# Sigmoid attention with a gated convolution: rounding of q and k in the DMA, tap products on GpSimd, due times anew

## The chip, the cores and the metric

The kernel runs on one core of one Trainium2 chip. The metric is the device time of one execution in microseconds, as the median of several runs. The engines are named as in the profile: PE is TensorE, PEld its weight loads, DVE is VectorE, ACT is ScalarE, POOL is GpSimd, SP is SyncE, which here only issues DMAs.

## What is computed

Attention with a sigmoid in place of the softmax, for 8 batches, 12 heads, 448 tokens and a head size of 64, and behind it a projection that is gated by a causal convolution of 5 taps over the tokens:

```python
scores = scale * np.matmul(q, k.transpose(0, 1, 3, 2)) - np.log(S)
attn = 1.0 / (1.0 + np.exp(-scores))
x = heads side by side of np.matmul(attn, v)          # [8, 448, 768]

for k in range(K):                                     # K = 5, x padded with zeros in front
    gate_pre += conv_w[k][None, None, :] * xp[:, k:k + S, :]
gate = 1.0 / (1.0 + np.exp(-gate_pre))
val = x @ w_val
return (gate * val @ w_out).astype(np.float32)
```

All inputs and outputs are fp32.

## The kernel before

**Tiling.** The 96 heads are taken in 48 pairs: pair i has two heads of 64 rows on the 128 partitions. Two pairs make a "two" j (24 of them), and three twos a batch (6 pairs of heads, 768 channels). Tokens lie along the free dimension. The first batch has no product of its own: its 448 tokens are dealt out to the other seven as an eighth segment of 64 tokens, so that each of seven batches has 512 tokens (line 654 loads that piece as x<-first_x).

**Precision.** PE multiplies fp32 slowly, so most operands are split in a rounded part and a remainder. The first 15 pairs are multiplied whole (`qk_single`, one L516 product). From pair 15 on, 33 pairs, q and k are split: `qk_hi` is the fp32r rounding of `qk_src`, `qk_lo` the remainder, and scores are three products. The sigmoid of the scores (L552) is split in two fp16 parts (`a`, L367 on ACT and L563 on DVE), v in `v_hi` and `v_lo`, x in `xs`, the gated value y in `g`, and the weights in `w_val_hi`, `w_val_lo`, `w_out_hi`, `w_out_lo`. The weights come as 64-bit words that three steps on DVE and ACT turn into fp32 (`w_words`), a maximum over each piece (`val_max`, `out_max`) gives its scale.

**Stages.** For each pair: load, split, scores (L516, and L539 for the last 64 tokens of both pairs of a two), sigmoid. For each two: the products with v (L602, L610) into `ps_a`, a copy of x out of PSUM, its maximum (`x_max`, L658), and the gate: the tap k=0 is a product x times conv_w that begins the gate; taps k=1 (and k=2 in the first gated batch) are added by DVE (L679); for the others (ADDED = 3, ADDED_FIRST = 2) a product is made in a `tap` tile, two instructions for a tile, and a DMA adds the tile to the gate (L683, on the POOL queue). Then a sigmoid of the gate (L685). For each batch: the maximum over x is spread over the partitions by a product with a diagonal (L702) and gives the scale of `xs`; then six `val` products (L753), y = value times gate (L777), the split of y in g, six `out` products (L753), and the stores.

**Order.** Nothing is left to a scheduler of the framework. Each piece of work is handed to `op` with the engines that may do it and a cost on each (`{"V": 0.31, "A": 0.45}`: DVE or ACT; G is POOL, S is SP), a due time, and the buffers it reads and writes. `Plan.issue` walks through planned time: an engine that is free takes the ready piece with the earliest due time, and DVE leaves a piece that ACT may also do if ACT is free within `AT["share"]`. The order found is written out for each engine; at run time each engine goes through its list in order and waits for semaphores. The due times are `tau(i)`, a clock of pairs, plus an offset from the table `AT`.

**Rings.** Buffers are reused in turn: `qk_src`, `qk_hi`, `qk_lo` have two each, `tap` two, `gate` four, `x` five, `ps_a` three, `ps_m` two, `w_words` three.

In the profile before, the casts are L361 (ACT) and L363 (DVE), the subtraction for qk_lo is L372 on POOL, and the tap products are `tap<-x,cw` at L367 on ACT.

Of the kernel before, what the change touches and what calls it, by code (L numbers as in the profile page):

```python
# [24 lines left out]
KT = 5  # L25
P = 128
# [52 lines left out]
    first=6.63, step=13.72, val=-77.5, val_step=60.94, out=57.5, out_step=597.15, w_max=-57.5,  # L79
    w_split=-155, load_qk_first=-152, load_qk=69.5, load_v=-40.5, split_hi=-2, split_lo=30,  # L80
    rest_first=95.5, rest=251, a_first=-174.5, a=-7, attend=-47.5, v_max=76.5, v_exp=14.5,
    v_split=-159.5, x=-174.5, x_max=-98, x_scale=-307, x_hi=52.5, x_lo=-185.5, x_step=2940.66, tap=51,
    scores=68.5, a_rest=85, a_rest_first=-72.5, tap_first=22, tap_pair=68.5, tap_step=56.18, gate=-110,
    product=63.5, y=-61.5, g_hi=186.5, g_lo=6, o=-97, share=0.3, w_load=-117,
# [39 lines left out]
class Op:  # L124
    __slots__ = ("ways", "prio", "emit", "deps", "n", "start", "end", "eng", "after", "size", "port", "then")

    def __init__(self, n, ways, prio, emit, size, port):
        self.n, self.ways, self.prio, self.emit, self.size, self.port = n, ways, prio, emit, size, port
        self.deps, self.after, self.then = set(), None, None
        self.start = self.end = self.eng = None  # L130
# [126 lines left out]
def attention_then_gate(  # L257
# [371 lines left out]
    def after(j):  # L629
# [318 lines left out]
```

## Time and profile before

| | |
|---|---|
| median of 3 runs | 579.03 us (578.53 to 579.27) |
| span of the profiled execution | 578.0 us |
| median less that span | 1.03 us |
| PE, DVE, ACT, POOL busy | 571.4, 428.4, 435.4, 138.2 us |
| DMA queue of SP (q1) | 56.37 MB, 28.9% of 16 engines |
| DMA queue of POOL (q0) | 31.46 MB, 29.4% of 16 engines |

The profile is one execution; its own time is its span and what lies around it, which for the median of the runs is 1.03 us. "Busy" is the time in which an engine has an instruction of its own; "idle before, releaser" in a group's row is how long the engine stood before these instructions and what let it go on. PE's matmuls overlap their neighbours, so a row's mean is longer than the step from one to the next.

### The profile page before, as it was taken

The page shows a single profiled execution, that of the slowest core. Times are in us where ns is not written, and L with a number is a line of the kernel's source. Part 1 is how long each engine was busy: PE and PEld are TensorE (multiplying, and loading weights), DVE is VectorE, ACT ScalarE, POOL GpSimd, SP SyncE. Part 2 cuts the span into 40 slices and gives each one's busy share as a digit, 9 for nine tenths or more (in the row PEclk, how much of TensorE's full clock was granted, in tenths as well). Part 3 has the DMA queues.
Part 4 walks back from the last instruction along what each step waited for, and adds up shares of the span by engine and source line. Part 5 has one row for each costly group of instructions (what it writes and reads, how often), then busy time and mean ns, then how long its engine had stood idle before and what let it go on. Part 6 is the DMA issues. An engine that isn't in the chain of part 4 may idle for free.

```text
span 578.0 us, 9459 instructions
## 1 busy us (share of the span) xinstructions
PE 571.4 (99%) x3592; PEld 280.2 (48%) x3592; DVE 428.4 (74%) x693; ACT 435.4 (75%) x579; POOL 138.2 (24%) x162
## 2 busy tenths in 40 slices
PE   9999999999999999999999999999999999999997
PEld 5343334455555555545555454554545555544444
DVE  1867999899977959888598886889777886760310
ACT  5677988879888869778697878788788897862112
POOL 0000203332424222243322333223322322110000
PEclk9999999999999999999999999999999999999999
DMA  8988677757484564825657364565635663355012
GB/s 327 355 279 267 174 210 188 203 120 184 124 215 83 146 157 141 207 58 155 136 158 176 102 169 96 166 156 155 169 74 168 155 133 74 72 128 129 2 37 74
DMA packets 39310, 88.44 MB, mean 153 GB/s; under 512 B 14944, under 2 KB 20448, under 8 KB 39264
## 3 DMA queue, kind: packets, MB, share of 16 engines
q0 software_dynamic: 8640, 31.46, 29.4%
q1 hardware_dynamic: 30624, 56.37, 28.9%
q8 instruction: 28, 0.46, 0.3%
q14 instruction: 18, 0.15, 0.1%
HBM read 43.96 MB, written 12.40 MB: 98 GB/s over the span
## 4 chain that ended last, share of the span: by engine, by line
PE 90%; DVE 5%; ACT 3%; DMA 1%; issue 1%; ACTq 0%; DVEq 0%
PE ps_m L753 54%; PE ps_a L516 15%; PE ps_a L610 14%; PE ps_a L539 3%; PE ps_a L602 2%; DMA gate<-tap 1%; ACT a_single L552 1%; DVE x_max L658 1%; DVE gate L679 1%; PE ps_m L800 1%; DVE a L563 1%; DVE w_words L389 1%; DVE out_max L415 0%; ACT tap L367 0%; ACT a L367 0%
## 5 line engine op out<-in xcount | busy, mean ns | idle before, releaser
L753 PE MATMUL ps_m<-g,w_out_hi 128*128 128x512 f16 (+1 forms) x516 | 150.5, 374 | 0.0
L753 PE MATMUL ps_m<-xs,w_val_hi 128*128 128x512 f16 x504 | 150.1, 379 | 0.0
L552 ACT ACTIVATE ps_a<-ps_a 128x896 f32<-128x896 f32 x112 | 99.3, 909 | 14.2 <-DVE v_exp L544 6.5
L563 DVE SCALAR_TENSOR_TENSOR a<-ps_a,a 128x896 f16<-128x896 f32 x96 | 100.8, 1082 | 7.0 <-ACT a L367 6.7
L372 POOL TENSOR_TENSOR qk_lo<-qk_src,qk_hi 128x448 fp32r<-128x448 f32 x66 | 75.2, 1151 | 119.8 <-ACT qk_hi L361 36.7
L753 PE MATMUL ps_m<-g,w_out_lo 128*128 128x512 f16 (+1 forms) x258 | 96.5, 374 | 0.0
L683 POOL DMA_DIRECT2D gate<-tap x60 | 53.5, 892 | 178.6 <-ACT tap L367 70.2
L753 PE MATMUL ps_m<-xs,w_val_lo 128*128 128x512 f16 x252 | 95.5, 379 | 0.0
L367 ACT ACTIVATE a<-ps_a 128x896 f16<-128x896 f32 x96 | 85.0, 927 | 0.2
L367 ACT ACTIVATE tap<-x,cw 128x512 f32<-128x512 f32 x120 | 82.2, 739 | 1.5 <-DMA gate<-tap 1.5
L753 PEld LDWEIGHTS <-w_out_hi 128*128 128x128 f16 x516 | 49.0, 98 | 59.6 <-issue 5.3
L753 PEld LDWEIGHTS <-w_val_hi 128*128 128x128 f16 x504 | 47.8, 98 | 61.1 <-issue 5.9
L777 DVE SCALAR_TENSOR_TENSOR y<-ps_m,y_scale,gate 128x512 f32<-128x512 f32 x42 | 29.9, 745 | 34.3 <-PE ps_m L753 34.3
L610 PE MATMUL ps_a<-a,v_hi 128*64 128x448 f16 x384 | 52.7, 354 | 0.0
L367 ACT ACTIVATE y<-ps_m,o_scale 128x512 f32<-128x512 f32 (+1 forms) x35 | 23.1, 678 | 38.0 <-PE ps_m L753 25.4
L552 ACT ACTIVATE a_single<-ps_a 128x896 f32<-128x896 f32 x56 | 48.0, 927 | 4.5 <-PE ps_a L516 4.1
L361 ACT CAST g<-y 128x512 f16<-128x512 f32 x28 | 17.2, 618 | 33.7 <-DVE y L777 32.9
L516 PE MATMUL ps_a<-qk_hi 64*128 64x448 f32 x198 | 39.8, 398 | 0.1
L753 PEld LDWEIGHTS <-w_out_lo 128*128 128x128 f16 x258 | 25.2, 98 | 29.2
L753 PEld LDWEIGHTS <-w_val_lo 128*128 128x128 f16 x252 | 24.7, 98 | 29.7
L516 PE MATMUL ps_a<-qk_single 64*128 64x448 f32 x180 | 39.0, 566 | 0.0
L610 PE MATMUL ps_a<-a_single,v_src 128*64 128x448 f32 x192 | 37.8, 543 | 0.0
(108 smaller groups left out, 752.9 us busy)
## 6 DMA issues: line engine op xcount, KB each, us to landing
gate<-tap POOLq DMA_DIRECT2D x60, 512.0 KB, 4.9
qk_src<-qk SPq DMA_DIRECT2D x33, 448.0 KB, 5.4
v_src<-vs SPq DMA_DIRECT2D x24, 448.0 KB, 4.3
out_t<-y SPq DMA_DIRECT2D x41, 224.0 KB, 3.1
qk_single<-qk SPq DMA_DIRECT2D x15, 448.0 KB, 5.9
w_words<-w_val SPq DMA_DIRECT2D x6, 768.0 KB, 8.1
w_words<-w_out SPq DMA_DIRECT2D x6, 768.0 KB, 5.4
x<-first_x SPq DMA_DIRECT2D x21, 68.0 KB, 4.2
```

The lines of the kernel that those rows point to most:

```text
L361: nc.scalar.copy(to, x)
L367: nc.scalar.activation(to, x, AF.Copy, scale=by)
L372: engines[eng].tensor_tensor(to, x, y, op=ALU.subtract)
L516: mm(b()[:, h, :S], k()[rows, at : at + P], q()[rows, :S], start=(n == 0), stop=(n == len(terms(i)) - 1))
L539: mm(b()[to, h, :S], x[n]()[rows, CW:], x[n]()[rows, :S], start=True, stop=True)
L552: nc.scalar.activation(to, b()[:, :, :S], AF.Sigmoid, bias=-math.log(S), scale=1.0 / math.sqrt(D))
L563: op({"V": 1.0}, t + 0.5, lambda e: nc.vector.scalar_tensor_tensor(part(1), p(), A_SCALE, part(0), op0=ALU.mult, op1=ALU.subtract), [b], [ ...
L602: mm(px()[to, p, :S], v()[rows, h * D : (h + 1) * D], x(s["a"])[rows, h, at : at + S], start=(j > 0 and n == 0), stop=(j == 0 and n == len ...
L610: mm(px()[to, p, :S], v()[:, o : o + D], x(st[2 * j + p]["a", c])[:, h, at : at + S], start=(j == 0 and c == 0 and n == 0), stop=(j > 0 an ...
L683: op({"G": 1.1}, at + AT["tap_step"] * k, lambda e, tap=tap: nc.gpsimd.dma_start(g(), tap(), accum_op=ALU.add), [tap], [g], 4 * P * T * 4, "")
L753: mm(po()[:, cs], w()[:, c, :], x(k)[:, cs], start=(c == 0 and j == 0), stop=(c == NC - 1 and j == 2))
L777: op({"V": 0.66}, t + AT["y"], lambda e: nc.vector.scalar_tensor_tensor(y(), po(), y_scale()[:, m : m + 1], gate()[:, m % 2, :], op0=ALU.m ...
```

## The change

Three things are changed.

- The rounded part `qk_hi` no longer is a cast of the loaded `qk_src` by DVE or ACT (two casts for each pair). A DMA on the POOL queue reads q and k from HBM a second time, fp32, and writes them as fp32r: one DMA for each of 33 pairs, 128 x 832 elements. `qk_src` is still loaded by SP, since the remainder and L539 read it.
- The products for the adding DMA, 120 of 128 x 512, are made by POOL with a `tensor_scalar` (times the weight, times 1.0), not by ACT. Their planned cost on POOL is `TAP_G`.
- The table `AT` has new values throughout, and due times are rounded to five places. `share`, 0.3 before, is 16.048: DVE takes a piece that ACT may do only if ACT is not free within 16 us of planned time.

```diff
+TAP_G = 0.65
...
 AT = dict(
-    first=6.63, step=13.72, val=-77.5, val_step=60.94, out=57.5, out_step=597.15, w_max=-57.5,
...
+    first=2.733, step=19.657, val=-59.018, val_step=26.262, out=78.183, out_step=3.48, w_max=-221.49,
...
-        self.n, self.ways, self.prio, self.emit, self.size, self.port = n, ways, prio, emit, size, port
+        self.n, self.ways, self.prio, self.emit, self.size, self.port = n, ways, round(prio, 5), emit, size, port
...
-        s["halves"] = (h, h.part()), (l, l.part())
-        for n, cs in enumerate((slice(0, S), slice(S, CW))):
-            op({"V": 0.31 - 0.03 * n, "A": 0.45 - 0.06 * n}, t + AT["split_hi"] + n, lambda e, cs=cs: copy(
-                e, h()[:, cs], x()[:, cs]), [x], [s["halves"][0][n]])
+        s["halves"] = (h,), (l, l.part())
+        op({"G": 1.0}, t + AT["split_hi"], lambda e: nc.gpsimd.dma_start(h()[:, :CW], qk[i][:, :CW]), [], [h], P * CW * 4, "")
         for n, cs in enumerate((slice(0, S), slice(S, CW))):
             op({"G": 1.13 - 0.14 * n}, t + AT["split_lo"] + n, lambda e, cs=cs: sub(
-                e, l()[:, cs], x()[:, cs], h()[:, cs].bitcast(F32)), [x, s["halves"][0][n]], [s["halves"][1][n]])
+                e, l()[:, cs], x()[:, cs], h()[:, cs].bitcast(F32)), [x, h], [s["halves"][1][n]])
...
-                    op({"A": 0.61}, at + AT["tap_step"] * k - AT["tap_first"] + AT["tap_pair"] * p, lambda e, p=p, k=k, tap=tap: scaled(
-                        e, by(tap()[:, p, :]), x()[:, p, :, HALO - k : HALO + SL - k], w(p, k)), [x, own, edge, cw], [tap])
+                    op({"G": TAP_G}, at + AT["tap_step"] * k - AT["tap_first"] + AT["tap_pair"] * p, lambda e, p=p, k=k, tap=tap: nc.gpsimd.tensor_scalar(
+                        by(tap()[:, p, :]), x()[:, p, :, HALO - k : HALO + SL - k], w(p, k), 1.0, op0=ALU.mult, op1=ALU.mult), [x, own, edge, cw], [tap])
```

**What moves.** PE's own order of scores, products with v, val and out stays nearly the same; only the small sums over a weight's maximum and the last out products shift by a group. The lists of the other engines change. The rows below are each engine's list: line, operation, output<-inputs, shape, and how many in a row. All lines from 79 on are one or two higher in the changed kernel.

The first place is ACT about the fourth two, where the sigmoids of whole scores (`a_single`) follow each other, three for each pair and one for the last tokens of both. Before:

```order
L361 COPY x_first<-ps_a 128x2x448
L552 ACTIVATE a_single<-ps_a 128x896 x3
L367 ACTIVATE w_val_hi_76<-w_words,val_scale 128x768
L552 ACTIVATE a_single<-ps_a 128x896 x3
L367 ACTIVATE w_words<-w_words 128x768
L552 ACTIVATE a_single<-ps_a 128x896
```

Now, at the same place (`w_val_hi_76` is the split of the fourth piece of w_val):

```order
L363 COPY x_first<-ps_a 128x2x448
L552 ACTIVATE a_single<-ps_a 128x896 x6
L369 ACTIVATE w_words<-w_words 128x768
L369 ACTIVATE w_val_hi_76<-w_words,val_scale 128x768
L369 ACTIVATE w_words<-w_words 128x768
L552 ACTIVATE a_single<-ps_a 128x896
```

The split stood between the third and fourth sigmoid and now stands behind the sixth, with two weight steps beside it.

The second place is ACT about the end of the first gated batch, where the copy of x of its third two and the diagonal are made (`diagonal` feeds PE's L702). Before:

```order
L367 ACTIVATE gate<-x,cw 128x512
L367 ACTIVATE tap<-x,cw 128x512
L552 ACTIVATE a_single<-ps_a 128x896
L367 ACTIVATE tap<-x,cw 128x512
L367 ACTIVATE w_words<-w_words 128x768
L361 COPY x<-ps_a 128x2x7x64
L552 ACTIVATE a_single<-ps_a 128x896 x2
L367 ACTIVATE diagonal<-eye,x_exp 128x128
L685 ACTIVATE gate<-gate 128x1024
L552 ACTIVATE a_single<-ps_a 128x896
L367 ACTIVATE gate<-x,cw 128x512
L552 ACTIVATE a_single<-ps_a 128x896 x3
```

Now:

```order
L369 ACTIVATE w_words<-w_words 128x768
L552 ACTIVATE a_single<-ps_a 128x896
L369 ACTIVATE w_words<-w_words 128x768
L369 ACTIVATE w_out_hi_79<-w_words,out_scale 128x768
L369 ACTIVATE gate<-x,cw 128x512
L363 COPY x<-ps_a 128x2x7x64
L552 ACTIVATE a_single<-ps_a 128x896 x2
L369 ACTIVATE diagonal<-eye,x_exp 128x128
L552 ACTIVATE a_single<-ps_a 128x896
L369 ACTIVATE w_out_hi_80<-w_words,out_scale 128x768
L552 ACTIVATE a_single<-ps_a 128x896 x3
L369 ACTIVATE gate<-x,cw 128x512
```

The taps are gone; a second weight step and the split `w_out_hi_79` stand ahead of the copy; behind the diagonal the gate's sigmoid and first product have made way for the split `w_out_hi_80`, and come later.

The third place is POOL in the steady rounds, in the middle of the run. Before:

```order
L372 TENSOR_TENSOR qk_lo<-qk_src,qk_hi 128x448
L372 TENSOR_TENSOR qk_lo<-qk_src,qk_hi 128x384
L683 DMA gate<-tap 128x1024
L372 TENSOR_TENSOR qk_lo<-qk_src,qk_hi 128x448
L372 TENSOR_TENSOR qk_lo<-qk_src,qk_hi 128x384
L683 DMA gate<-tap 128x1024 x2
L372 TENSOR_TENSOR qk_lo<-qk_src,qk_hi 128x448
L372 TENSOR_TENSOR qk_lo<-qk_src,qk_hi 128x384
L683 DMA gate<-tap 128x1024
```

Now, one round but for its first rounding DMA:

```order
L683 DMA gate<-tap 128x1024
L676 TENSOR_SCALAR tap<-x,cw 128x512 x2
L374 TENSOR_TENSOR qk_lo<-qk_src,qk_hi 128x448
L374 TENSOR_TENSOR qk_lo<-qk_src,qk_hi 128x384
L676 TENSOR_SCALAR tap<-x,cw 128x512
L683 DMA gate<-tap 128x1024
L676 TENSOR_SCALAR tap<-x,cw 128x512
L491 DMA qk_hi<-qk 128x832
L683 DMA gate<-tap 128x1024
L676 TENSOR_SCALAR tap<-x,cw 128x512 x2
L374 TENSOR_TENSOR qk_lo<-qk_src,qk_hi 128x448
L374 TENSOR_TENSOR qk_lo<-qk_src,qk_hi 128x384
```

The rounding DMA (L491) and the taps (L676) stand between the adding DMAs and the subtractions, in the same queue.

More of the change, by code (lines that the diff above doesn't have):

```diff
@@ L78 @@
 AT = dict(
-    first=6.63, step=13.72, val=-77.5, val_step=60.94, out=57.5, out_step=597.15, w_max=-57.5,
[L80 to L84, printed above, removed]
+    first=2.733, step=19.657, val=-59.018, val_step=26.262, out=78.183, out_step=3.48, w_max=-221.49,
+    w_split=33.386, load_qk_first=104.807, load_qk=20.792, load_v=-68.68, split_hi=-198.804, split_lo=134.64,
+    rest_first=127.881, rest=74.399, a_first=-78.558, a=100.55, attend=12.316, v_max=-132.349, v_exp=38.626,
+    v_split=14.892, x=-171.861, x_max=6.222, x_scale=-195.085, x_hi=167.921, x_lo=-101.178, x_step=-61.033,
+    tap=139.978, scores=-32.37, a_rest=-86.907, a_rest_first=83.495, tap_first=52.395, tap_pair=44.824,
+    tap_step=13.244, gate=-122.307, product=-110.026, y=187.474, g_hi=-107.116, g_lo=-182.634, o=161.052,
+    share=16.048, w_load=150.276,
 )
```

## The prediction

> **What bounds the kernel now.** I read the busy times first, then the work by stage, then what TensorE waits for, then the order of time at the places where it waits.
>
> ```profile
> span 578.0 us, 9459 instructions
> ...
> PE 571.4 (99%) x3592; PEld 280.2 (48%) x3592; DVE 428.4 (74%) x693; ACT 435.4 (75%) x579; POOL 138.2 (24%) x162
> ```
>
> TensorE (PE) works 571.4 of 578.0 us. The stages, cut where its idle time begins and ends (columns: stretch, length, busy PE, PEld, DVE, ACT, POOL, then granted clock, DMA share, GB/s):
>
> ```profile
> 44.00:46.00 2.00, 1.70 (x14) 0.41 (x12) 2.00 (x3) 2.00 (x3) 0.69 (x1) 1.00 0.66 204
> ...
> 74.00:83.00 9.00, 7.69 (x48) 2.60 (x43) 9.00 (x22) 8.28 (x11) 0.88 (x1) 1.00 0.84 243
> 83.00:150.00 67.00, 66.89 (x402) 31.76 (x394) 62.65 (x106) 57.71 (x80) 20.76 (x23) 1.00 0.69 169
> 150.00:574.22 424.22, 424.22 (x2729) 215.99 (x2728) 306.26 (x471) 315.35 (x423) 110.55 (x121) 1.00 0.53 128
> 574.22:578.00 3.78, 0.00 (x0) 0.00 (x0) 0.00 (x0) 0.47 (x1) 0.00 (x0) 1.00 0.21 65
> ```
>
> The reader is to see three things. The clock is full. From 150 to 574 PE has no gap at all, so nothing that makes another engine lighter saves time there; it can only lose some. And the idle time that can be won is small: 578.0 - 571.4 is 6.6 us, of which 3.78 is the end (the last result on its way out) and 1.1 the start (first row below); the other 1.7 us lie between 44 and 150, 0.30 and 1.31 of them in the first two stretches.
>
> What PE waits for, over the whole run (total, times, longest):
>
> ```profile
> PE ps_m L800 <- DVE ones L793: 1.1, 1, 1.1
> PE ps_a L702 <- ACT diagonal L367: 0.9, 1, 0.9
> PE ps_a L539 <- ACT a_single L552: 0.7, 2, 0.4
> ```
>
> The last two rows are two places at which ScalarE (ACT) is late. The earlier, in order of time (start, length):
>
> ```profile
> 41.12 2.54 ACT L552 ACTIVATE a_single<-ps_a 128x896 f32<-128x896 f32 x3
> ...
> 43.53 1.02 ACT L367 ACTIVATE w_val_hi<-w_words,val_scale 128x768 f16<-128x768 f32 x1
> ...
> 44.46 2.52 ACT L552 ACTIVATE a_single<-ps_a 128x896 f32<-128x896 f32 x3
> ...
> 45.42 0.98 PE L539 MATMUL ps_a<-qk_single 64*64 64x448 f32 x8 [0.30 <-ACT a_single L552]
> ```
>
> A weight's split stands between the third and the fourth of six sigmoids and takes 44.46 - 43.53 = 0.93 us of ACT; PE wants the buffer that the fourth frees. The later:
>
> ```profile
> 69.72 0.76 ACT L367 ACTIVATE gate<-x,cw 128x512 f32<-128x512 f32 x1
> ...
> 74.70 0.93 ACT L367 ACTIVATE w_words<-w_words 128x768 f32<-128x768 f32 x1 [2.18 <-DVE w_words L389]
> ...
> 75.51 0.90 ACT L361 COPY x<-ps_a 128x896 f32<-128x896 f32 x1
> ...
> 76.62 1.21 DVE L658 TENSOR_REDUCE x_max<-x 128x2 f32<-128x1024 f32 x1
> ...
> 78.06 0.40 ACT L367 ACTIVATE diagonal<-eye,x_exp 128x128 bf16<-128x128 bf16 x1
> 78.37 1.04 ACT L685 ACTIVATE gate<-gate 128x1024 f32<-128x1024 f32 x1
> 78.51 0.22 PE L702 MATMUL ps_a<-diagonal,ones 128*128 128x64 bf16 x2 [0.91 <-ACT diagonal L367]
> ...
> 80.11 0.71 ACT L367 ACTIVATE gate<-x,cw 128x512 f32<-128x512 f32 x1
> ...
> 81.68 0.59 PE L539 MATMUL ps_a<-qk_single 64*64 64x448 f32 x2 [0.39 <-ACT a_single L552]
> ```
>
> x is copied 0.8 us late (75.51), behind a weight step that itself waited for DVE; so its maximum, the diagonal and PE's L702 are late: 0.91. Then three steps that are no sigmoid (diagonal, a gate's sigmoid, a gate's first product) stand before the fourth sigmoid, and PE waits 0.39 more.
>
> **The change, part by part.** Costs come from these groups and queues (mean ns of one; share of 16 DMA engines; us from issue to landing):
>
> ```profile
> L367 ACT ACTIVATE tap<-x,cw 128x512 f32<-128x512 f32 x120 | 82.2, 739 | 1.5 <-DMA gate<-tap 1.5
> L683 POOL DMA_DIRECT2D gate<-tap x60 | 53.5, 892 | 178.6 <-ACT tap L367 70.2 <-DVE gate L679 29.6 <-ACT y L367 21.5
> L372 POOL TENSOR_TENSOR qk_lo<-qk_src,qk_hi 128x448 fp32r<-128x448 f32 x66 | 75.2, 1151 | 119.8 <-ACT qk_hi L361 36.7
> L372 POOL TENSOR_TENSOR g<-y,g 128x512 f16<-128x512 f32 x6 | 7.0, 1159 | 13.5 <-ACT g L361 13.5
> L369 DVE TENSOR_SCALAR gate<-x,cw 128x512 f32<-128x512 f32 x22 | 10.1, 478 | 0.0
> L363 DVE CAST qk_hi<-qk_src 128x384 fp32r<-128x384 f32 x24 | 15.6, 650 | 0.0
> ...
> q0 software_dynamic: 8640, 31.46, 29.4%
> q1 hardware_dynamic: 30624, 56.37, 28.9%
> ...
> gate<-tap POOLq DMA_DIRECT2D x60, 512.0 KB, 4.9
> ```
>
> *The casts of q and k* leave DVE (46 of them, about 24 us) and ACT (20, about 11 us). In their place come 33 DMAs on the POOL queue, 128 x 832 x 4 = 426 KB each: 33 x 0.892 = 29.4 us of issuing, and transfers at a speed that no row shows. Bounds: q1 moves 56.37 MB in 28.9% of 578 us, 337 GB/s, so 1.26 us for one; q0, which adds, 185 GB/s, so 2.30 us. I take the second, the same queue: 76 us in all, 13% more of the DMA engines, none of which PE waits for now. Each rounding DMA waits for a buffer that PE frees, and behind it on POOL wait adding DMAs and subtractions. With two buffers and two score groups in a PE round of 24.8 us (below), a buffer is free 12 us before its next use; issue, landing (4.9, as the adding DMA) and two subtractions take 8.1. Term 0. SP keeps its loads; the first weight is now loaded behind one load of v more, 1.4 us by q1's speed, and PE asks for its sum only behind the third group of scores: 0.
>
> *The 120 tap products* leave ACT (82.2 us) for POOL. No row shows a one-input product there. Upper bound: POOL's two-input subtraction of 512 columns, 1.16 us; lower: DVE's product of the same shape, 0.48. I take 0.75, between, since one of two inputs is gone: 90 us. The Trainium skill (GPSIMD Engine Reference, section 4.1, Engine selection) has one-input work on GpSimd at roughly line rate; by the 1.03 cycles for an element at 1.2 GHz of the same page, an estimate is 0.44 us and 53 us in all, by which the total would not differ.
>
> POOL's sum: 138.2 + 29.4 + 90 + 2.3 (two subtractions of g more) = 260 us, 45%; at 1.16 it is 309, 53%. Its queue is in order, so the round counts, which PE repeats every 24.8 us:
>
> ```profile
> 159.90 0.91 PE ps_a L539 x8
> ...
> 184.71 0.91 PE ps_a L539 x8
> ```
>
> A round holds 6 taps, 3 adding DMAs, 2 rounding ones and 4 subtractions: 6 x 0.75 + 5 x 0.892 + 4 x 1.151 = 13.6 us. The second and the third adding DMA also wait for the landing of the one before, 4.9 - 0.9 = 4.0 us each if nothing is put in between: 21.6 of 24.8. It fits: 0.
>
> *Due times.* By a count of instructions the work that both could do goes to ACT: the 22 first gate products (10.5 us of DVE, 16 of ACT at the tap's 739 ns) and 61 more of 0.5 to 1.2 us (v_hi, xs, y, g, weights). With the casts, I estimate DVE at 350 us, and ACT at 435 - 82 - 11 + 71 = 413. Both stay below PE, so this is worth only what it does at the two places:
> - First place: the weight splits stand behind the six sigmoids. The 0.30 goes (bounds 0 and 0.30).
> - Second place: before x's copy stand a weight step, a sigmoid, a weight step, a split and a gate product, 0.8 + 0.8 + 0.8 + 0.9 + 0.6 = 3.9 us after a sixth sigmoid that ends at about 69.9; done at 73.8, before PE is done with that x at 74.7. So the copy can start 0.7 us earlier. DVE, busy 9.00 of 9.00, must have its weight steps done by then, so I give half of the 0.91 back, 0.45 (bounds 0 and 0.91). Before the fourth sigmoid stand the diagonal and one split of 0.93, no longer the diagonal, a sigmoid (0.94) and a product (0.61): 0.30 of the 0.39 goes (bounds 0 and 0.39).
> - A new wait: the first gate's sigmoid now stands between the second and third xs on ACT and waits for an adding DMA, with xs, x's copy and the sigmoids behind it. That DMA stands in the POOL queue about a PE group (12 us) earlier and lands in 4.9: 0.
> - Against that: POOL computes from 54 us on beside a full DVE. I put down 0.2 us (bounds 0 and 1.5, second rival).
>
> Sum: 0.30 + 0.45 + 0.30 - 0.20 = 0.85 us. The profiled span 578.0 becomes 577.15. The median of the runs, 579.03, lies 1.03 above that span, so I expect 578.2. A measurement of this kernel can tell about 0.2% (1.16 us) from no change; this sits inside.
>
> **The rivals.**
>
> *All the idle time goes.* 1.7 us are won, not 0.85: 577.3, faster. For it: DVE gets 78 us lighter, ACT's steps stand in better places. Against: x's maximum is still behind weight steps on a DVE without slack.
>
> *POOL blocks DVE, and DVE eats the gain.* DVE's L387 beside a subtraction on POOL, and alone:
>
> ```profile
> 68.57 1.14 POOL L372 TENSOR_TENSOR qk_lo<-qk_src,qk_hi 128x448 fp32r<-128x448 f32 x1 [3.63 <-PE ps_a L516]
> ...
> 68.79 1.34 DVE L387 TENSOR_SCALAR w_words<-w_words 128x768 int32<-128x768 uint32 x1
> ...
> 80.69 0.55 DVE L387 TENSOR_SCALAR w_words<-w_words 128x768 int32<-128x768 uint32 x1
> ```
>
> It ends only after POOL's has: 0.79 us lost. Between 54 and 77 us stand some six new taps and the two subtractions; two such hits ahead of x's maximum are 1.5 us, the diagonal's wait is back and longer: 578.5 to 579.9, no change. The Trainium skill (SBUF — State Buffer, section Who interferes with whom) says that the two engines share a port pair, which one of them holds for a whole instruction while the other is blocked. The two rows agree with it. Against: the casts, often hit themselves (650 ns for 384 columns), are gone.
>
> *POOL's queue becomes the bound: slower.* Place: the rounds from 150 on, where PE has no slack. A round takes 9.1 + 8.0 us + 6 taps; it passes 24.8 when a tap takes over 1.28 us and nothing fills the waits. At 1.5 it is 1.3 us a round, over 14 rounds 18 us: 597. It needs a tap dearer than the two-input row. A small form lies in the first batch: the second adding DMA of its third gate (before at 103.89) now stands behind a subtraction of g that waits for a y (107.90), and that gate is used at 125.29:
>
> ```profile
> 103.89 0.87 POOL L683 DMA_DIRECT2D gate<-tap  x1
> ...
> 107.90 1.41 DVE L777 SCALAR_TENSOR_TENSOR y<-ps_m,y_scale,gate 128x512 f32<-128x512 f32 x2 [1.34 <-PE ps_m L753]
> ...
> 125.29 1.40 DVE L777 SCALAR_TENSOR_TENSOR y<-ps_m,y_scale,gate 128x512 f32<-128x512 f32 x2
> ```
>
> Before, 125.3 - 103.9 - 4.9 = 16.5 us are free; some 9 of them go. Beyond the rest each us is lost once: 580.5 to 583.
>
> **How the numbers follow.** My forecast (most of the two places won, 577.5 to 579.0) has 0.50; all won or more (577.5 or less) 0.16; DVE blocked 0.19; POOL late in the first batch 0.09; POOL the bound 0.06. Faster by over 0.2% is under 577.9: the second case and a little under half of the first, 0.38. Slower is over 580.2: the last two and a rest, 0.16. Between: 0.46. The range, 576.8 to 581.0, leaves out the bound POOL and the far ends.
>
> **What would show it.** Right: PE's wait for a_single at 45 us gone, the one for the diagonal under 0.6 us, no idle PE after 150, POOL 230 to 290 us busy, taps of 0.5 to 1.1 us, DVE near 350 and ACT near 413. Wrong: a tap above 1.3 us; PE waiting for qk_lo, or y for a gate; the rounding DMA landing much later than 5 us after its issue, with subtractions waiting behind it; DVE's weight steps stretched between 55 and 80 us.

## The result, and the profile after

The changed kernel takes 588.24 us (median of 4 runs, 586.38 to 589.33) where the kernel before takes 579.15 (4 runs beside it, 578.53 to 579.58): 1.0152 times as long, 95% interval 1.0132 to 1.0172. The forecast was 578.2, no change; it became slower by 9 us. The profiled execution is the 586.38 one. The page of the kernel after, busy times and DMA queues:

```profile
span 584.6 us, 9435 instructions
...
PE 571.8 (98%) x3592; PEld 280.9 (48%) x3592; DVE 378.7 (65%) x561; ACT 415.2 (71%) x523; POOL 249.9 (43%) x317
...
q0 software_dynamic: 13392, 45.52, 36.7%
q1 hardware_dynamic: 30624, 56.37, 29.4%
```

PE's matmuls are the same, and its busy time too (571.8 us, 571.4 before), so most of the 6.6 us that the span grew is idle time of PE or a low clock. DVE lost 50 us of busy time, and the kernel became slower all the same. What the two moved operations cost, by groups and DMA issues:

```profile
L676 POOL TENSOR_SCALAR tap<-x,cw 128x512 f32<-128x512 f32 x120 | 107.8, 935 | 51.1 <-DMA gate<-tap 31.5
...
L491 POOL DMA_DIRECT2D qk_hi<-qk x33 | 20.1, 609 | 100.1 <-PE ps_a L516 95.7
...
gate<-tap POOLq DMA_DIRECT2D x60, 512.0 KB, 5.4
...
qk_hi<-qk POOLq DMA_DIRECT2D x33, 416.0 KB, 3.7
```

What PE waits for (total, times, longest). The first two rows are new:

```profile
PE ps_a L536 <- DVE a L563: 4.2, 1, 4.2
PE ps_m L753 <- DVE y L777: 1.7, 2, 0.9
PE ps_m L800 <- DVE ones L793: 1.1, 1, 1.1
PE ps_a L702 <- ACT diagonal L369: 0.8, 1, 0.8
PE ps_a L539 <- ACT a_single L552: 0.5, 2, 0.2
```

Where the time goes is read by the start of the same matmul in both traces. The first fence is of the kernel before, the second of the kernel after; in each the first row stands at the end of the first gated batch, the second at the first steady round:

```profile
83.41 4.73 PE L610 MATMUL ps_a<-a_single,v_src 128*64 128x448 f32 x24
159.83 0.98 PE L539 MATMUL ps_a<-qk_src 64*64 64x448 f32 x8
```

```profile
80.67 4.73 PE L610 MATMUL ps_a<-a_single,v_src 128*64 128x448 f32 x24
165.83 0.98 PE L539 MATMUL ps_a<-qk_src 64*64 64x448 f32 x8
```

At 83 us the changed kernel is 2.7 us ahead (about 1 us of it from the first 10 us, where PE's clock happened to rise earlier; the same code began up to 0.3 us behind in another run), at 160 us 6.0 behind, and it stays there: to the end of PE's work the lag moves by 0.2. Then the end is 0.8 us longer (4.53 us behind the last product, against 3.78). All of the loss but these 0.8 us so lies between 83 and 145 us. The stretches of the kernel after (columns as in the prediction):

```profile
97.00:101.00 4.00, 2.27 (x15) 1.08 (x12) 3.95 (x14) 1.32 (x3) 1.70 (x2) 1.00 0.00 0
101.00:133.00 32.00, 32.00 (x180) 15.20 (x179) 27.30 (x40) 25.18 (x32) 20.48 (x25) 1.00 0.83 203
133.00:138.00 5.00, 0.81 (x5) 0.20 (x3) 5.00 (x5) 1.91 (x3) 1.99 (x2) 0.92 0.37 104
138.00:145.00 7.00, 7.00 (x49) 3.14 (x51) 4.16 (x8) 2.76 (x3) 2.27 (x3) 0.57 0.64 188
145.00:574.00 429.00, 429.00 (x2751) 217.17 (x2748) 269.78 (x379) 305.14 (x386) 199.54 (x250) 1.00 0.64 157
```

Three losses, as the start of the same matmul falls behind: 1.8 us at 97 to 101; 4.35 at 133 to 138; and from 138 to 145, where PE is never idle, but at a granted clock of 0.57, 2.6 more. The large one, in order of time, on DVE, then on POOL, then on PE:

```profile
130.00 0.60 DVE L464 TENSOR_SCALAR o_base<-out_inverse,y_inverse 128x6 f32<-128x6 f32 x1
130.64 4.39 DVE L720 TENSOR_SCALAR o_scale<-o_base,x_exp 128x6 f32<-128x6 f32 x1
134.95 1.94 DVE L448 SCALAR_TENSOR_TENSOR w_out_lo<-w_words,out_scale,w_out_hi 128x768 f16<-128x768 f32 x2
136.81 2.08 DVE L563 SCALAR_TENSOR_TENSOR a<-ps_a,a 128x896 f16<-128x896 f32 x2
```

```profile
129.73 0.88 POOL L683 DMA_DIRECT2D gate<-tap  x1 [1.18 <-DMA gate<-tap]
130.38 0.97 POOL L676 TENSOR_SCALAR tap<-x,cw 128x512 f32<-128x512 f32 x1
131.04 1.26 POOL L374 TENSOR_TENSOR qk_lo<-qk_src,qk_hi 128x384 fp32r<-128x384 f32 x1
132.02 0.94 POOL L676 TENSOR_SCALAR tap<-x,cw 128x512 f32<-128x512 f32 x1
132.68 2.32 POOL L374 TENSOR_TENSOR qk_lo<-qk_src,qk_hi 128x448 fp32r<-128x448 f32 x2
```

```profile
137.94 0.19 PE L536 MATMUL ps_a<-vm,ones 128*128 128x1 bf16 x1 [4.19 <-DVE a L563]
138.06 1.77 PE L539 MATMUL ps_a<-qk_src 64*64 64x448 f32 x8
```

A scaling of six numbers for a partition, `o_scale`, takes 4.39 us on DVE. It ends (135.03) as POOL's row of two taps and three subtractions ends (135.00). Behind it stand two weight splits and only then `a`, for which PE has been waiting since 133.8. Then PE's first matmuls last 1.77 us instead of the 0.98 in the steady round: the low clock. At 98 PE waits twice for `y`, 0.8 and 0.9 us. A `gate` product of DVE ahead of them lasts 2.19 us beside POOL, but weight steps and reductions stand ahead of both `y` too; which of the two it is, this trace doesn't tell.

### The profile page after: what moved, and what is told of

Its sections match the earlier page's. It is cut to its first block, busy times and chain, and to the rows that moved or that the text cites. A ratio compares the mean times of both kernels' runs of the same rounds, so it can differ in the third digit from the quotient of the medians.

```text
span 584.6 us, 9435 instructions
## 1 busy us (share of the span) xinstructions
PE 571.8 (98%) x3592; PEld 280.9 (48%) x3592; DVE 378.7 (65%) x561; ACT 415.2 (71%) x523; POOL 249.9 (43%) x317
## 3 DMA queue, kind: packets, MB, share of 16 engines
q1 hardware_dynamic: 30624, 56.37, 29.4%
## 4 chain that ended last, share of the span: by engine, by line
PE 88%; DVE 7%; ACT 2%; DMA 1%; issue 1%; DVEq 0%; ACTq 0%
PE ps_m L753 52%; PE ps_a L516 15%; PE ps_a L610 14%; PE ps_a L539 4%; PE ps_a L602 2%; DMA w_words<-w_out 1%; DVE w_words L414 1%; DVE out_max L417 1%; DVE gate L679 1%; DVE w_out_lo L448 1%; PE ps_m L800 1%; DVE vm L531 1%; DVE y L777 0%; ACT a L369 0%; ACT ps_a L552 0%
## 5 line engine op out<-in xcount | busy, mean ns | idle before, releaser
L676 POOL TENSOR_SCALAR tap<-x,cw 128x512 f32<-128x512 f32 x120 | 107.8, 935 | 51.1 <-DMA gate<-tap 31.5
L363 ACT CAST g<-y 128x512 f16<-128x512 f32 x42 | 25.8, 615 | 63.6 <-DVE y L777 63.3
L683 POOL DMA_DIRECT2D gate<-tap x60 | 52.8, 879 | 42.3 <-DVE gate L679 20.1
L491 POOL DMA_DIRECT2D qk_hi<-qk x33 | 20.1, 609 | 100.1 <-PE ps_a L516 95.7
L369 ACT ACTIVATE y<-ps_m,o_scale 128x512 f32<-128x512 f32 (+1 forms) x43 | 28.2, 678 | 40.5 <-PE ps_m L753 30.7
L610 PE MATMUL ps_a<-a,v_hi 128*64 128x448 f16 x384 | 53.9, 362 | 0.0
L658 DVE TENSOR_REDUCE x_max<-x 128x2 f32<-128x1024 f32 x21 | 25.6, 1218 | 33.4 <-ACT x L369 32.4
L679 DVE SCALAR_TENSOR_TENSOR gate<-x,cw,gate 128x512 f32<-128x512 f32 x48 | 42.3, 894 | 0.0
L753 PEld LDWEIGHTS <-w_out_lo 128*128 128x128 f16 x258 | 25.3, 98 | 29.2
```

Source lines behind the costliest of these rows:

```text
L363: nc.scalar.copy(to, x)
L369: nc.scalar.activation(to, x, AF.Copy, scale=by)
L610: mm(px()[to, p, :S], v()[:, o : o + D], x(st[2 * j + p]["a", c])[:, h, at : at + S], start=(j == 0 and c == 0 and n == 0), stop=(j > 0 an ...
L676: op({"G": TAP_G}, at + AT["tap_step"] * k - AT["tap_first"] + AT["tap_pair"] * p, lambda e, p=p, k=k, tap=tap: nc.gpsimd.tensor_scalar(by ...
L679: op({"V": 0.67}, at + AT["tap_step"] * k + AT["tap_pair"] * p, lambda e, p=p, part=part, k=k: nc.vector.scalar_tensor_tensor(part(), x()[ ...
L683: op({"G": 1.1}, at + AT["tap_step"] * k, lambda e, tap=tap: nc.gpsimd.dma_start(g(), tap(), accum_op=ALU.add), [tap], [g], 4 * P * T * 4, "")
```

## The experiments

All times are medians in us, the ratio is to the kernel before, run beside it on the same chip (579.15 to 579.80). The column "expected" is the time that the theory under test gave before the run (of the first theory, where there were two).

| | what | expected | time | ratio, 95% |
|---|---|---|---|---|
| after | the change | 578.2 | 588.24 | 1.0152 (1.0132 to 1.0172) |
| e1 | `a` first on DVE | 581.3 | 583.43 | 1.0078 (1.0050 to 1.0106) |
| e2 | POOL's row later | 581.5 | 581.78 | 1.0034 (1.0019 to 1.0050) |
| e3 | before, new due times alone | 577 to 580 | 613.37 | 1.0585 (1.0556 to 1.0613) |
| e4 | after, due times of before | 581 to 592 | 590.45 | 1.0187 (1.0157 to 1.0216) |
| e5 | e2, `y` first at 97 us | 578.2 | 583.46 | 1.0075 (1.0062 to 1.0088) |
| e6 | before, rounding DMA alone | 577.5 to 580 | 582.20 | 1.0059 (1.0043 to 1.0074) |
| e7 | before, taps on POOL alone | 582 to 592 | 600.89 | 1.0373 (1.0357 to 1.0390) |
| e11 | after, copies that let DVE in | 579 to 582 | 581.25 | 1.0038 (1.0023 to 1.0053) |
| e12 | e11, due times of before | 580 to 586 | 585.08 | 1.0098 (1.0085 to 1.0112) |
| e13 | after, both places of DVE's order | 580 | 584.13 | 1.0079 (1.0058 to 1.0100) |
| e14 | e11 and e13 together | 578 | 582.98 | 1.0055 (1.0043 to 1.0068) |
| e15 | e14, two loads of v later | 581 | 578.96 | 0.9992 (0.9983 to 1.0001) |
| e16 | before, copies | 578.5 | 579.15 | 0.9992 (0.9983 to 1.0001) |

**e1 and e2: is it the held instruction?** e1 leaves POOL alone and puts DVE's three `a` ahead of the weight steps. e2 leaves DVE alone and makes POOL begin its row only when the second split is done, by a small copy that reads it:

```diff
 DVE's list (e1)
+L563 SCALAR_TENSOR_TENSOR a<-ps_a,a x3
 L464 o_base, L720 o_scale, L448 w_out_lo x2
-L563 SCALAR_TENSOR_TENSOR a<-ps_a,a x3
 e2
+        if o.n == 634:
+            nc.gpsimd.tensor_copy(passed(), w_lo["out", 5]()[:, 0, :2])
```

> The changed kernel, in which VectorE's row at the end of the first batch is put in another order: the three attention products (a) stand ahead of o_base, o_scale and the two splits w_out_lo, not behind them; GpSimd's row is untouched. Theory 1 (VectorE is held by GpSimd: o_scale, an instruction of 0.2 us, took 4.39 us because GpSimd ran one instruction after another from 130.4 to 135.0; the 4.19 us of TensorE's wait and the low clock of some 6 us after it, about 2.7 us, both follow from it): o_scale is still held for about 4 us, but nothing that TensorE needs stands behind it; TensorE waits under 0.5 us there, its clock stays full, and the time is 588.2 - 4.2 - 2.7 = 581.3 (580 to 582.5). Theory 2 (the due times: the weight steps in front of the a's are the delay, whatever GpSimd does): the same time, 581, but o_scale takes 0.2 to 0.6 us. Rival (the clock falls for a reason of its own, as by the load): the wait goes, the low clock stays, 584.

> The changed kernel with one small copy more on GpSimd, ahead of the tap product at 130.4 us; it reads the second split w_out_lo, so that GpSimd's run of five instructions starts only when VectorE has done o_scale and both splits. VectorE's order stays as it was. Theory 1 (held by GpSimd): o_scale takes 0.2 to 0.3 us, the a's come 4 us earlier, TensorE waits 0.2 to 1 us there, the clock stays full: 581.5 (580 to 583). Theory 2 (the order of VectorE alone): the a's still stand behind o_scale and two splits, TensorE still waits 3 us or more: 586 or more.

In both the wait at 134 us and the low clock behind it are gone, and 4.8 and 6.5 of the 9.1 us come back. In e2 the scaling is (first row) 0.23 us long. It is 0.23 in e1 too, not the 4 that were expected: there it starts at 137.03, when POOL's row has just ended, and during the row DVE had nothing to do but wait for ACT. So e1 does not tell the hold from the order. e2 does: DVE's order is as in the changed kernel, and without the hold the wait is gone. e1 is also 2 us slower than expected, for in both another hold, at 93 us, is longer than it was; the second row is of e2, the third of e1 in a fence of its own:

```profile
133.00 0.23 DVE L720 TENSOR_SCALAR o_scale<-o_base,x_exp 128x6 f32<-128x6 f32 x1
...
92.73 3.14 DVE L391 TENSOR_SCALAR w_words<-w_words 128x768 int16<-128x768 int16 x1
```

```profile
93.26 3.51 DVE L679 SCALAR_TENSOR_TENSOR gate<-x,cw,gate 128x512 f32<-128x512 f32 x1
```

These take 1.03 and 0.73 us alone. The waits for `y` at 100 us grow with them, from 1.7 to 2.2 (e2, with 1.6 us of low clock behind them) and 2.6 (e1, with the clock full). Which DVE instruction is hit is a matter of tenths of a microsecond between two queues.

**e3, e4, e6, e7: the parts.** The due times alone (the table `AT` of after in before, and the reverse), the rounding DMA alone, the tap products alone (both with the due times of before):

> The kernel before with the new due times alone: casts of q and k on VectorE and ScalarE, tap products on ScalarE. Theory 1 (held by GpSimd): GpSimd is busy about 140 us as before and has no run of five compute instructions beside weight steps, so TensorE has no wait over 1 us after 60 us: 577 to 580. Theory 2 (due times): TensorE waits at the end of the first batch as in the changed kernel, 583 to 588.

> The changed kernel with the due times of before: rounding by DMA and tap products on GpSimd stay. Theory 1 (held by GpSimd): GpSimd is busy about 250 us as in the changed kernel, so VectorE's instructions are held in the first batch too (where they are held, the plan does not tell); TensorE waits for VectorE by a few us, 581 to 592. Theory 2 (due times): no more waits than before, 577 to 580.

> The kernel before with the rounding DMA alone: its due times, its tap products on ScalarE. Theory 1 (GpSimd's compute instructions hold VectorE): GpSimd gets some 20 us of issuing and no compute, VectorE and ScalarE lose 35 us of casts; no new wait of TensorE: 577.5 to 580. Rival (the rounding DMA is itself late, and the subtractions behind it): TensorE waits for qk_lo, 582 or more.

> The kernel before with the tap products alone on GpSimd: its due times, its casts of q and k. Theory 1: GpSimd computes about 190 us and VectorE still has its casts, which are held too; VectorE's busy time grows by 20 us or more by holding alone, and TensorE waits for it in the first batch, by 3 to 10 us with the low clock after it: 582 to 592. Rival (the tap products are harmless where VectorE has not been made lighter): 577.5 to 580.

No part is a gain. e3 says little of the two theories and missed both: with `share` at 16 the planner gives ACT the casts and taps that after no longer has there, and ACT is busy 512.8 us (84%). The due times belong to the new division of work; without them the other two parts are no better (e4). e6 and e7 do tell: each brings holds of its own. In e6 a `w_out_lo` split lasts 3.26 us at 73 (0.99 alone), behind an adding DMA and POOL's row; PE waits 1.8 for the diagonal, 0.9 before, and the clock is low behind it (0.81 from 74 to 83 us). So its time is that of the rival, but for another reason: PE never waits for `qk_lo`. Some 35 us of casts less on DVE and ACT brought nothing. In e7 one split lasts 5.05 us, PE waits 11.1 us for `xs`, and the time is above the expected range.

**e8, e9, e10: what holds DVE, and for how long.** Microbenchmarks that compute nothing of the reference. DVE does one instruction while POOL runs a row of products of 512 columns (the tap) and subtractions of 448; with or without an adding DMA issued ahead of the row; with or without a copy of one column in it that reads the result before it. e8 also lets PE stand idle for set times.

> None of the reference is computed, zeros are written. Two things are measured by themselves. First, eight forms of VectorE instruction, each alone and beside 1, 2 and 4 GpSimd instructions in a row (a tap product of 512 columns, then subtractions of 448). Theory 1 (VectorE is held until GpSimd's whole run has ended): the scaling of 128 x 6 takes 0.23 us alone, and 0.5, 1.2 and 3 us or more beside 1, 2 and 4; so does what reads two operands from SBUF; what reads PSUM, a reduction and a 128 x 1 step are not held. Rival (held for one GpSimd instruction at most): the same time beside 2 and 4 as beside 1 or 2, about 1 us. Second, TensorE's 512-column matmuls after idle times of 0.6 to 6 us. If idle time lowers the clock: steps of 216 ns after short ones, and 427 ns for some us after those above 3 to 4 us, 2 to 3.5 us lost each. If the low clock after the wait had another reason, all steps stay at 216 ns.

> None of the reference is computed, zeros are written. GpSimd runs four instructions in a row (a tap product of 512 columns and a subtraction of 448, twice; each into a tile of its own, so that none waits for anything inside the row: 3.6 us by 0.69 and 1.13 each), four times by themselves and four times right behind an adding DMA of GpSimd's; VectorE issues one instruction into this (the scaling of 128 x 6, or the split of 128 x 768 with two operands from SBUF) after 3, 5, 7 or 9 steps of 128 x 1. In the run before, where the second GpSimd instruction waited for a semaphore, VectorE got in behind the first one (0.46 us). Theory 1a (a row without a wait inside holds VectorE to its end): 1.5 to 3.5 us for the scaling, with and without the DMA. Theory 1b (the DMA's descriptors, written by GpSimd, hold it): 0.5 us without the DMA, 3 us or more behind it. Rival (one GpSimd instruction at most, here too): up to 1.2 us in every case, and then the 4.39 us in the changed kernel are something else.

> None of the reference is computed, zeros are written. The scaling of 128 x 6 on VectorE into GpSimd's row of four again, after 7, 9 and 11 steps, in five forms: without a DMA; behind an adding DMA (both as in the run before: under 1.2 us, and about 3.5 us); with a small memset between the DMA and the row; with a 128 x 1 copy behind the first instruction that reads its result, and so waits for its end; with such a copy behind each. If GpSimd keeps the port only while it starts each instruction before the last one has ended (their records overlap by 0.3 us behind a DMA, by 0.03 us otherwise), a wait inside the row lets VectorE in: 0.3 to 1.3 us with a copy behind each, and with one behind the first alone 1.3 us, or 2.5 if the row then overlaps again; the memset changes nothing, 3.5. If the DMA itself holds VectorE for its time, all four forms with a DMA give 3 us or more.

Without a DMA an instruction is held to the end of the running POOL instruction and no longer, as the rival of e8 had it. In e8 the 128x6 scaling takes 0.22 us alone and 0.39 to 0.47 beside one to four of them; a cast of 512 columns 0.42 and 0.72; a gate product 0.74 and 0.98. In e9, whose rows have no wait inside, the scaling takes at most 0.91 and the split at most 1.69 (1.01 alone). A 128x1 step (0.20), `a`, which reads PSUM (1.08), and a reduction (0.94) are never held in e8. Behind an adding DMA (e9) the same scaling takes 3.20 and 3.56 us, the split 3.98 and 4.35: both end with the whole row of four. That is so in the two tries of each in which it starts into the running row; in the other two it starts just ahead of the row's first product and is not kept (scaling 0.34 and 0.67, split 1.07 and 1.44). The scaling in e10 without a DMA, behind one, and behind one with a copy after the first product:

```profile
11.04 0.53 DVE L102 TENSOR_SCALAR six_o<-c,c 128x6 f32<-128x6 f32 x1
...
26.25 3.20 DVE L102 TENSOR_SCALAR six_o<-c,c 128x6 f32<-128x6 f32 x1
...
63.17 0.35 DVE L102 TENSOR_SCALAR six_o<-c,c 128x6 f32<-128x6 f32 x1
```

A memset between the DMA and the row does nothing (3.23 at the same place). Behind a DMA the records of POOL's instructions overlap by 0.3 us (0.94 to 1.00 for a product that takes 0.69 otherwise, the next starting after 0.66), which is a part of the tap's mean of 935 ns. That POOL does not let go of the shared port between two such instructions fits this; the records do not show the port itself. A copy that has to wait for the result before it ends the row for DVE.

PE's idle time and what follows, in e8 (64 matmuls, 13.99 us at full clock):

```profile
234.00 13.99 PE L144 MATMUL to<-x,w 128*128 128x512 f16 x64 [1.52 <-ACT w L142]
250.12 15.67 PE L144 MATMUL to<-x,w 128*128 128x512 f16 x64 [2.13 <-ACT w L142]
268.55 15.55 PE L144 MATMUL to<-x,w 128*128 128x512 f16 x64 [2.75 <-ACT w L142]
```

A gap of 1.52 us costs nothing more (twice of two). One of 2.13 cost 1.68 us more in both tries, 2.75 and 3.37 in one of two each, 3.98 and 5.22 in the one try of each. So a wait of 4.19 us costs itself and a second price behind it.

The granted clock in the kept traces shows why one gap costs more and the next does not. It changes only at steps of 3.41 us, counted from its first rise; in the changed kernel it is 0.50 from 137.20 to 144.03, two such steps. A step at full clock in which PE is idle for 2.03 us or more is followed by one at 0.50 in every trace; with 1.76 or less it never is; of the three between, 1.78 (e6) is, 1.89 (e8) and 1.91 (e3) are not. So a gap that falls across the border of two steps may cost only itself: e1's two waits at 100 us, 1.7 in one step and 0.9 in the next, did; e2's, 1.3 and 0.9 in one step, did not.

**e11, e12, e16: letting DVE in.** A copy of one column on POOL behind the first computing instruction after each DMA:

```diff
+        if o.eng == "G" and o.size:
+            behind_dma = True
+        elif o.eng == "G" and o.result and behind_dma:
+            result = o.result()
+            nc.gpsimd.tensor_copy(read[result.dtype](), result)
+            behind_dma = False
```

> The changed kernel, all orders as they are, with one small copy on GpSimd behind the first compute instruction after each of its DMAs; it reads one column of that instruction's result, and so waits for its end. Theory 1 (behind its own DMA GpSimd runs on without letting VectorE in, until something in its row waits): o_scale takes under 1.3 us instead of 4.39, no VectorE instruction of the first batch is held by more than 1.4 us, TensorE's wait at 134 us is under 0.7 us and its clock stays full there: 588.2 - 3.7 - 2.7 = 581.8 at most; with the smaller holds near 92 us the wait at 98 us shrinks too, by up to 1.7: 579 to 582. Rival (the order of the due times is the main loss): the waits at 98 and 134 us stay above 1.5 and 2.5 us, 585 or more. Rival (some 0.4 us more of GpSimd for each DMA delay its chain): new waits for gates or qk_lo, 583 or more.

> The same copies, in the changed kernel with the due times of before (590.45 without them, with a wait of 5.4 us for xs near 97 us). Theory 1: most of VectorE's 51 us of holding goes, the wait for xs falls under 3 us: 580 to 586. Rival (the old due times are wrong for the new work, whatever holds VectorE): the wait for xs stays over 4 us, 588 to 592.

> The kernel before with the copies on GpSimd that let VectorE in, nothing else. Theory 1: VectorE's holding falls from 25 us to under 18, above all at 70 us (1.96 for 0.59) and 128.6 us (2.54 for 0.41); the weight steps ahead of x's maximum end 1 to 1.5 us earlier and TensorE's wait for the diagonal, 0.91, goes: 578.5, faster by 0.2% (0 to 0.3). Rival (nothing of what is held there is on the path): 579.2 to 580.

e11 takes back 7.0 of the 9.1 us with nothing else changed: no held instruction is longer than 2.1 us in the first 160 us, and the clock is full throughout. Two waits remain, 1.7 us for `y` at 100, where less was expected, and 1.2 for `a` at 135. With the due times of before the same copies give 585.08 (590.45 without them): the wait for `xs` at 98 is 4.9 us where it was 5.4. That an order made for other work is behind it was not tried. In the kernel before they change nothing: DVE is held some 25 us in all there too (25.3 and 24.7 us over the shortest of each form), once for 2.1 us more than its own time, at 128.6, but never on PE's path.

**e5, e13, e14, e15: the order, and what is late next.** e5 is e2 with the two `y` at 97 us ahead of a weight step, a gate product and two reductions. e13 is after with the two `y` ahead of the reductions there, and with e1's edit; e14 is e13 with e11's copies:

```diff
 DVE's list at 97 us (e13, e14)
+L777 SCALAR_TENSOR_TENSOR y<-ps_m,y_scale,gate x2
 L417 TENSOR_REDUCE out_max<-w_words
-L777 SCALAR_TENSOR_TENSOR y<-ps_m,y_scale,gate
 L531 TENSOR_REDUCE vm<-v_src
 L399 TENSOR_SCALAR out_inverse<-ps_a
-L777 SCALAR_TENSOR_TENSOR y<-ps_m,y_scale,gate
 L399 TENSOR_SCALAR out_inverse<-ps_a
```

> The changed kernel mended at both places where TensorE waited: at the end of the first batch GpSimd's run waits for VectorE's second split (as in the run with GpSimd later), and near 97 us VectorE does the two products y that TensorE waits for ahead of a weight's joining (w_words), a gate step and a maximum, not behind them. Theory 1 (instructions held by GpSimd, and what stands behind them in VectorE's row, are the whole loss): no wait of TensorE over 0.7 us after 60 us, the clock stays full, and what the due times won before 82 us, 1.6 to 1.8 us, is left: 579.5 - 1.2 = 578.2 (577.5 to 579). Rival (the weight steps put back are now late themselves): a new wait of 1 to 2 us between 105 and 126 us, 579 to 581.

> The changed kernel with VectorE's order mended at both places and nothing else: at 98 us the two products y stand ahead of a weight's maximum and v's maximum, and at the end of the first batch the attention products a stand ahead of o_base, o_scale and the two splits. GpSimd still holds VectorE behind its DMAs. Theory 1 (the holding delays whatever stands in the row): the wait near 98 us falls from 2.8 to about 1.5 us, one of 2 us there may still lower the clock; 588.2 - 7 - 1.3 = 580 (579 to 583). Rival (the order is the loss): no wait over 0.5 us at either place, 577.5 to 578.5.

> The same order and the copies on GpSimd that let VectorE in. Theory 1 (holding and order together are the whole loss): no wait of TensorE over 0.7 us between 90 and 150 us, the clock full; of the 2.2 us that the new due times had won at 82 us most is left: 581.25 - 1.9 - 1.4 = 578 (577.3 to 579), faster than before by 0.2%. Rival (a third delay stands behind, as after the earlier mend at 98 us, where a gate came late): a new wait of 1 us or more between 100 and 150 us, 579 to 581.

In e5 and e14 the wait at 98 is gone, and PE starts the next part earlier only to wait at 126 (e5 3.9, e14 1.9 us). So e5 is no faster than e2, nor e14 than e11, and e5, e13 and e14 are all 4 to 5 us slower than expected. e13 shows the hold once more, on another instruction (first row, 0.72 alone). In e14 (second row) the gate's sigmoid on ACT waits 3.44 us for an adding DMA, and the sigmoid of scores and `a` stand behind it:

```profile
131.03 4.87 DVE L679 SCALAR_TENSOR_TENSOR gate<-x,cw,gate 128x512 f32<-128x512 f32 x1
```

```profile
121.24 1.06 ACT L687 ACTIVATE gate<-gate 128x1024 f32<-128x1024 f32 x1 [3.44 <-DMA gate<-tap]
```

That DMA was issued at 112.5 and landed at 121.2, 8.7 us where the median is 5.3. Its stretch before, and in e14 (next to last column: share of the DMA engines):

```profile
108.00:116.00 8.00, 8.00 (x56) 3.42 (x56) 7.21 (x13) 6.77 (x10) 1.51 (x1) 1.00 0.83 276
116.00:124.00 8.00, 8.00 (x44) 3.78 (x41) 7.97 (x12) 6.51 (x9) 2.39 (x3) 1.00 0.54 122
```

```profile
108.00:116.00 8.00, 8.00 (x50) 3.77 (x47) 7.61 (x12) 6.20 (x8) 6.06 (x8) 1.00 1.00 276
116.00:124.00 8.00, 7.84 (x44) 3.96 (x42) 2.72 (x3) 4.55 (x7) 3.44 (x7) 1.00 1.02 243
```

The DMA engines are full from 108 to 124 us: two loads of v (issued at 112.7) and the rounding DMAs run beside the adding one. Full engines alone are not it: in the changed kernel their share there is 1.00 and 0.99, and the same DMA lands in 5.5 us. There the two loads were issued 1.0 us behind it, in e14 and e5 (9.0 us) within 0.2 us of it. e15 is e14 with these two loads behind an `a` of ACT that ends at about 119 us, by a small transfer on SP's queue that reads it:

```diff
+        if o.n == 29:
+            nc.sync.dma_start(held(), products[656]()[:, 0, :64])
```

> The kernel with order and copies mended, in which the two loads of v at 112.7 us wait for an attention product of ScalarE's at about 118 us (by a small DMA on SyncE's queue that reads it). Theory 3 (the DMA engines are full, and the loads, which start earlier when TensorE is earlier, take the adding DMA's time): it lands 5 to 5.5 us after its issue, the sigmoid runs at 118 us, TensorE's wait of 2 us at 126 us is under 0.5; v comes later, which may cost up to 1 us at 128 us: 583 - 2 = 581 (580 to 582). Rival (the adding DMA is late for another reason): it still lands after 8 us or more, and the time is 583 or more.

The adding DMA, issued at 114.7, now lands in 4.7 us, the sigmoid does not wait, the wait at 126 is gone, and e15 is as fast as the kernel before (0.9983 to 1.0001), some 3.7 us under e14 by the two ratios. What stands behind the loads on SP's queue comes later with them. In its profiled run, one of the longer of 10 (580.20), a wait of 1.6 us stands at 89.6 us, again behind a sigmoid that waited for an adding DMA. No version was faster than before by more than the measurement can tell.

## Why the prediction was wrong, step by step

- *What bounds the kernel*: right. From 145 us PE has no gap in either kernel, and nothing that was saved on DVE (50 us) or ACT (20 us) saved time. The row for 83 to 150 us showed DVE at 62.65 of 67 us, an engine with no room just where PE reads from it; I read PE's 66.89 there and left the stretch.
- *The casts and the rounding DMA*: right in its sum of 0. Issue 0.609 us (0.892 taken), landing 3.7 (4.9). "None of which PE waits for" holds for the rounding DMAs themselves. Their transfers took 7 points of the DMA engines' time, not 13. What was not looked at is the adding DMA beside them: in runs that mend the hold or the order it comes late (e5, e14).
- *The taps*: 0.69 us each when not behind a DMA, a mean of 0.935 (0.75 taken); POOL 249.9 us (260 forecast). That it is so near is in part luck: the taps took 107.8 us where 90 were put down, the issues of the rounding DMAs 20.1 where 29.4. The queue is not the bound; that rival fell.
- *Due times*: in PE's waits they brought less than forecast. The 0.30 at 45 us is gone, but waits of 0.21 and 0.24 for the same sigmoids stand in the next two rounds (the 0.5 above); the diagonal's wait is 0.81, where it was to be under 0.6; the 0.39 is gone. All in all 0.4 us less of waiting by 83 us, where 1.05 was forecast. The lead is larger all the same: in e1 and e2, which start level, 1.5 and 1.8 us are won between 22 and 82 us. Some 1.25 us of it is in no wait. PE's own groups are shorter there: 24 score products run through in 4.78 us, where the kernel before ran two halves of 2.53 with a weight's small sum between. That shift was seen and not priced, so the size of the lead is luck. DVE 378.7 us instead of 350: the rows that it kept last some 16 us longer than before, 6.3 of it the gate products and 5.9 `o_scale`. Holding, measured over the shortest of each form, is 27.0 us, hardly more than before (25.3). ACT 415.2 (413).
- ***The term that failed***: "Against that: POOL computes from 54 us on beside a full DVE. I put down 0.2 us (bounds 0 and 1.5, second rival)." That POOL holds DVE was right; for how long, where, and what follows was wrong. I priced a hit by one row, 0.79 us, held to the end of one instruction of POOL, and looked for it from 54 to 77 us. `o_scale` lasts 4.39 us at 130, since behind a DMA the hold lasts for the whole row of POOL, and the change puts taps, subtractions and DMAs into such rows. The sum had no place for the clock either: 4.35 us of wait were followed by 2.6 of low clock, 7.0 us in the place of 0.2. The 1.8 at 98 had no term at all, since the stretch from 83 us on was left; moving `y` ahead takes that wait away (e13, e14), letting DVE in does not (e11, 1.7). Together 8.8 us, against the 2.7 won until then. The other runs of after had a mean granted clock of 0.991 where the profiled one had 0.994; on 585 us that is about the 1.8 us between it and the median.
- *What lies around the span*: the 1.03 us is the offset of a median to another run's span. In the profiled run of after it is 586.38 - 584.6 = 1.78. An error of 0.7 us.
- *The rival "POOL late in the first batch"*: a gate late by an adding DMA did come, but only in runs that mend the hold or the order (e5, e14).

So the cause of the 9 us is this, as far as it is shown. Rows of POOL behind a DMA hold DVE, where weight steps stand ahead of `a`: e2 and e11 take the hold away, e1 and e13 the order, and in each most of the 7 us at 133 to 145 come back. The order that puts reductions ahead of `y` is the 1.8 at 98 (e13, e14); whether holding has a part in it is open. The late adding DMA is no part of the 9 us: it comes up only when the others are mended (e5, e14), and e15, which issues two loads of v later, removes it. The parts don't add up: copies and order together (1.0055) are no faster than the copies alone (1.0038), and the intervals overlap. Still open: how POOL keeps the port behind a DMA, the 0.8 us at the end, and whether e15 needs all of its edits, which were not tried apart.

## What to carry to other kernels

Work moved to an idle GpSimd is not free for a VectorE that is near full: look at the stretch, not the run, and price the longest row of GpSimd instructions that stands behind one of its own DMAs, for VectorE's casts, scalings and steps with two SBUF operands (reductions, one-column steps and a step that reads PSUM were not held in e8). Where TensorE waits directly on VectorE, put the steps it waits for ahead of those that nobody needs yet, or break the row with a tiny instruction that waits for the result before it. A wait of TensorE of about 2 us or more is to be priced with a low clock behind it, 1.7 us for each step of 3.41 us at half clock; whether a wait near 2 us brings it depends on where it falls.

## What the runs showed of the hardware

- An instruction of VectorE was held by up to 4.2 us by one row of GpSimd behind its DMA (a scaling that takes 0.22 us alone took 4.39 in the changed kernel, and 2.81 to 3.70 in e9 and e10 where it started into a row of four), by at most 0.7 us without a DMA (0.91 for 0.22 in e9). The Trainium skill (SBUF — State Buffer, section Who interferes with whom) says that the loser of the shared port pair is blocked for the whole instruction of the other. The runs without a DMA agree (the 0.91 us end with the instruction of GpSimd that was running); behind a DMA the hold was over four or five instructions, and the measurement decides.
- The granted clock of TensorE fell after a gap of 2.13 us, in two of two tries, for 1.7 us lost. The Trainium skill (TensorE: Matmul & The Clock Gate, section What's actually happening) gives an idle window of about 3.4 us; here the gap that does it is shorter: idle for 2.03 us of a step of 3.41 us was always enough, 1.76 us never.
- A DMA that rounds fp32 to fp32r, 416 KB, issues in 0.61 us and lands in 3.7; one that adds, 512 KB, in 5.4, and in 8.7 and 9.0 with two loads of 448 KB issued within 0.2 us of it.
